# A prologue's order of steps: V weights later in TensorE's queue, the second weight spread as a step

## Chip, cores and metric

One core of a Trainium2 chip. The metric is the device time of one execution in microseconds; the time before is the median of 4 runs, 819.42 us (818.78 to 820.4). One execution was profiled.

## What is computed

x is 2048 tokens by 640, bf16. It is layer-normalised, goes through 32-head attention (20 channels a head) and through a gated unit, and both are combined with x:

```
xn  = layernorm(x)
q, k, v = xn @ wqkv                    # 32 heads of 20
s   = softmax(q k^T / sqrt(20)) v @ wo
g   = silu((sigmoid(xn @ w_gate) * (xn @ w_up)) @ w_down)
out = x + s * g
```

## The kernel before

The heads are taken in 8 groups of four (`GH`), the queries in 4 chunks of 512 tokens; a block is one group with one chunk. The kernel has two stages.

**The prologue** (the `with` that begins at line 259) normalises all of x, transposes it, and makes for group 0 the whole of K, the first chunk of Q, and V of tokens 0 to 1023 (for groups 0 and 1). Tokens lie in 16 tiles of 128; four tiles make a chunk. Transfers are issued by SyncE (SP) at lines 263 to 267: tiles 0 to 7, the q and k weights of group 0 (`wst`), tiles 8 to 15, the V weights (`wv0`). Everything else is a list of steps written out by hand, `PRO` (line 76): each entry names an engine, a step and its numbers, and line 404 issues them one after the other. Within an engine the list is the order of execution (the engines named in `manual_schedule`); an engine waits at a step until that step's inputs are there, whatever stands behind it. The steps:

- `st k` (lines 320 to 332): mean and variance of tile k, on VectorE (DVE) by two batch-norm statistics and an aggregate, or on ScalarE (ACT) by two activations with sums.
- `rs g` (334): reciprocal deviations of tiles 2g and 2g+1, on GpSimd (POOL); `xn k` (341): the normalised tile, on DVE.
- `tr k` (348): five 128x128 transposes on TensorE (PE) into one of four buffers `tp`; `ev k` (353): its copy into `xnT`, on ACT or DVE.
- `k c` (357): K of chunk c, five matmuls of 512 columns into the one buffer `pk`; `km c` (361): its largest absolute value per row, DVE; `kt c` (366): its copy to `kT`, ACT, behind `km c` by a wait on the same buffer. `k c+1` needs both done.
- `v c i` (379): V of two tiles, ten matmuls of 160 columns with `wv0` into one of two buffers `pv`; `ve c i` (383): its copy, ACT.
- `q`, `abs`, `mdp`, `md`, `bound`, `qe0` (369 to 397): the first chunk of Q, its absolute value, a bound on the scores from the largest k, and the copy of q. `qe0` is the last step; the first scores need it.
- `w0`, `idt`, `ones`, `consts`, `more1`, `more2`: constants on POOL; `warm` (315): 28 matmuls on tile 4 whose result is not used.
- `spread` (291): POOL copies the landed `wst` of group 0 into the padded tile `wqks[0]` that `k` and `q` read. `spread_wst` (187) and `load_wst` (181) do this for any group; `wst` has one buffer.

**The loop** (line 1063 on) is planned in Python while the program is built: a model of engine times, which starts at zero whatever the prologue took, hands out scores, exponentials, products with V, the gated unit and the output projection. The instruction order that comes of it is fixed. In its first round, at block 0, it calls `spread_wst(1, load_wst(1))` (line 1137). POOL and SP are not under the manual order there; in the built program this copy stands on POOL right behind `more2`, ahead of `rs 5`, `rs 4`, `rs 7` and `rs 6`, and its two transfers stand on SP right behind `wv0`.

Of the kernel before, what the change touches and what calls it, by code (L numbers as in the profile page):

```python
# [13 lines left out]
ACT = mybir.ActivationFunctionType  # L14
# [12 lines left out]
PG = 2  # L27
# [47 lines left out]

PRO = (
    ("ACT", "table"), ("POOL", "w0"), ("POOL", "idt"), ("POOL", "more1"), ("ACT", "st", 0), ("DVE", "st", 1),
    ("POOL", "ones"), ("POOL", "consts"), ("DVE", "st", 2), ("DVE", "st", 3), ("ACT", "st", 4), ("PE", "warm"),
    ("DVE", "st", 5), ("POOL", "rs", 0), ("ACT", "st", 6), ("DVE", "st", 7), ("POOL", "rs", 2), ("DVE", "xn", 1),
    ("DVE", "xn", 0), ("POOL", "rs", 1), ("PE", "tr", 1), ("DVE", "xn", 4), ("ACT", "st", 9), ("PE", "tr", 0),  # L80
    ("DVE", "xn", 5), ("PE", "tr", 4), ("DVE", "ev", 1), ("PE", "tr", 5), ("POOL", "rs", 3), ("DVE", "ev", 0),
    ("DVE", "xn", 2), ("PE", "v", 0, 0), ("DVE", "xn", 3), ("ACT", "ev", 4), ("POOL", "spread"), ("DVE", "st", 11),
    ("PE", "tr", 3), ("ACT", "ev", 5), ("PE", "tr", 2), ("DVE", "xn", 6), ("POOL", "more2"), ("ACT", "ev", 3),
    ("PE", "v", 1, 0), ("DVE", "st", 10), ("ACT", "ev", 2), ("PE", "tr", 6), ("ACT", "st", 15), ("DVE", "st", 13),
    ("PE", "q"), ("POOL", "rs", 5), ("DVE", "xn", 7), ("PE", "k", 0), ("DVE", "st", 8), ("ACT", "ve", 1, 0),
    ("ACT", "ev", 6), ("PE", "tr", 7), ("DVE", "xn", 11), ("POOL", "rs", 4), ("PE", "v", 0, 1), ("ACT", "ve", 0, 0),
    ("DVE", "km", 0), ("ACT", "ev", 7), ("DVE", "xn", 10), ("PE", "tr", 11), ("ACT", "kt", 0), ("DVE", "st", 14),
    ("PE", "v", 1, 1), ("ACT", "ve", 0, 1), ("ACT", "st", 12), ("PE", "k", 1), ("DVE", "xn", 8), ("POOL", "rs", 7),
    ("DVE", "ev", 11), ("DVE", "xn", 9), ("PE", "tr", 8), ("DVE", "km", 1), ("PE", "tr", 10), ("PE", "tr", 9),
    ("ACT", "ev", 8), ("DVE", "xn", 15), ("POOL", "rs", 6), ("DVE", "ev", 10), ("ACT", "kt", 1), ("PE", "tr", 15),  # L90
    ("DVE", "ev", 9), ("ACT", "ve", 1, 1), ("DVE", "xn", 14), ("ACT", "ev", 15), ("PE", "k", 2), ("DVE", "xn", 13),
    ("DVE", "xn", 12), ("ACT", "abs"), ("PE", "tr", 13), ("DVE", "km", 2), ("PE", "tr", 14), ("ACT", "ev", 13),
    ("PE", "tr", 12), ("DVE", "ev", 14), ("ACT", "kt", 2), ("DVE", "ev", 12), ("DVE", "mdp"), ("PE", "k", 3),
    ("DVE", "km", 3), ("ACT", "kt", 3), ("DVE", "md"), ("PE", "bound"), ("DVE", "qe0"),
)

LOG2E = 1.4426950408889634
# [14 lines left out]
def kernel(  # L112
# [68 lines left out]
    def load_wst(g):  # L181
        st = wk.tile([P, KD, 2, GC], BF16, tag="wst", bufs=1, name="wst")
        for t in range(2):
            nc.sync.dma_start(out=st[:, :, t, :], in_=wqkv_v[:, :, t, g * GC:(g + 1) * GC])
        return st

    def spread_wst(g, st):
        nc.gpsimd.tensor_copy(out=wqks[g % 2][:, :, :, 1:1 + DH],
                              in_=st.rearrange("p kd t (j e) -> p (kd t) j e", e=DH))
# [4 lines left out]
    def load_wv(pr):  # L194
        w = wk.tile([P, KD, 2 * GC], BF16, tag="wv", bufs=1, name="wv")
        nc.sync.dma_start(out=w, in_=wqkv_v[:, :, 2, pr * 2 * GC:(pr + 1) * 2 * GC])
        return w
# [61 lines left out]
    with tc.tile_pool(name="ln", bufs=2) as lp, \  # L259
# [14 lines left out]
        mdp = lp.tile([P, P], BF16, tag="mdp", bufs=1, name="mdp")  # L274
# [16 lines left out]
        def s_spread(eng):  # L291
            spread_wst(0, wst0)

        def s_consts(eng):
            nc.gpsimd.memset(vts[0].rearrange("p t h c -> p (t h) c")[:, :, 0:1], 1.0)
            nc.gpsimd.memset(esum, -1.0)
            esum_v = esum.rearrange("p (j i) -> p j i", i=32)
            nc.gpsimd.affine_select(out=esum_v, in_=esum_v, compare_op=ALU.is_ge, fill=0.0,
                                    base=0, pattern=[[-32, GH], [-P, 32]], channel_multiplier=1)
            nc.gpsimd.affine_select(out=esum_v, in_=esum_v, compare_op=ALU.is_ge, fill=0.0,  # L300
                                    base=31, pattern=[[32, GH], [P, 32]], channel_multiplier=-1)
# [94 lines left out]
        def s_qe0(eng):  # L396
            q_evac(pq[0], qts[0])

        nc.vector.memset(eps_t, 0.0)
        nc.vector.memset(mhalf, -0.5)  # L400
        steps = dict(table=s_table, idt=s_idt, w0=s_w0, ones=s_ones, spread=s_spread, consts=s_consts, more1=s_more1,
                     more2=s_more2, warm=s_warm, st=s_st, rs=s_rs, xn=s_xn, tr=s_tr, ev=s_ev, k=s_k, km=s_km, kt=s_kt,
                     mdp=s_mdp, md=s_md, v=s_v, ve=s_ve, q=s_q, abs=s_abs, bound=s_bound, qe0=s_qe0)
        for eng, name, *args in PRO:
            steps[name](eng, *args)

# [60 lines left out]
    def gc(b):  # L467
        if b < PAIR:
            return divmod(b, NQC)
        return NG - 2 + (b - PAIR) % 2, (b - PAIR) // 2  # L470
# [348 lines left out]
    for b in range(NBLK):  # L819
        g, c = gc(b)  # L820
# [242 lines left out]
    with tc.manual_schedule(engines={ENG.PE, ENG.Activation, ENG.DVE}):  # L1063
# [64 lines left out]
        while chain or items or glu_items or o_next < NQC or any(it.i < len(it.ops) for it in active):  # L1128
# [3 lines left out]
            if bb > blk_loaded:  # L1132
                blk_loaded = bb
                rule.update(zip(KEYS, PLAN[bb]) if bb < len(PLAN) else ())
                g, c = gc(bb)
                if c == 0 and g + 1 < PG:
                    spread_wst(g + 1, load_wst(g + 1))
                if c == 0 and g + 1 < NG:
                    if g % 2 == 1:
                        wvs[(g + 1) // 2] = load_wv((g + 1) // 2)  # L1140
# [39 lines left out]
            for eng in ("ACT", "DVE"):  # L1180
# [67 lines left out]
                elif pass_ok:  # L1248
                    dve_last = "pass"
                    d = dve_pass[0]  # L1250
                    k = d["k"]
# [199 lines left out]
```

## Time and profile before

| | |
|---|---|
| median of 4 runs | 819.42 us |
| profiled execution | 818.78 us |
| its span, first to last instruction | 816.8 us |
| PE, DVE, ACT, POOL busy | 776.1, 785.7, 782.9, 82.2 us |
| first scores start | 31.39 us |
| granted TensorE clock, mean | 0.993 |

Times in rows are microseconds from the span's start. In a timeline row the first number is the start, the second how long the group lasted, and the bracket holds the idle time of the engine before it and what ended it. In the chain of waits, each piece is a start, a length and what ran. In a table of windows each stretch has the busy time (and count) of PE, weight loads, DVE, ACT and POOL, then the granted clock, the transfer engines' share and GB/s. L numbers are lines of the kernel.

### The profile page before, as it was taken

The numbers are of one execution on the slowest core, as the hardware profiler recorded it, in microseconds if no ns is written. First come the engines' busy times: TensorE is split into PE (matmuls) and PEld (weight loads), VectorE is DVE, ScalarE is ACT, GpSimd is POOL, SyncE is SP. The second block draws the span as 40 slices with busy tenths as digits, with TensorE's granted clock in tenths as the row PEclk, the third lists the DMA queues.
The fourth block names the chain that finished last, engine by engine and source line by source line (L and its number), as shares of the span: only waits on it lengthen the run. The fifth ranks groups of instructions, "written<-read, shape, count | busy, mean of one in ns | idle before, by whom it ended". The sixth has DMA issues, their size and how long they took to land.

```text
span 816.8 us, 17041 instructions
## 1 busy us (share of the span) xinstructions
PE 776.1 (95%) x6456; PEld 271.7 (33%) x6456; DVE 785.7 (96%) x1244; ACT 782.9 (96%) x1008; POOL 82.2 (10%) x99
## 2 busy tenths in 40 slices
PE   5799999999999999999999999999999999998996
PEld 5433333333323323333333222333332223233332
DVE  7899999999999999999999999999999999998993
ACT  7899999999999999999999999999999999998991
POOL 6000000001000000000000010000000003022041
PEclk9999999999999999999999999999999999999999
DMA  5431311133222222322122222334121334315031
GB/s 159 138 79 51 100 38 36 41 76 84 66 68 70 60 56 73 81 56 76 46 59 65 71 84 62 85 111 118 44 86 40 93 90 133 98 54 149 25 101 40
DMA packets 95874, 62.57 MB, mean 77 GB/s; under 512 B 36388, under 2 KB 89684, under 8 KB 95792
## 3 DMA queue, kind: packets, MB, share of 16 engines
q1 hardware_dynamic: 95504, 61.16, 26.9%
q8 instruction: 50, 0.82, 0.4%
q14 instruction: 32, 0.26, 0.1%
q10 hardware_dynamic: 288, 0.33, 0.1%
HBM read 47.82 MB, written 13.63 MB: 75 GB/s over the span
## 4 chain that ended last, share of the span: by engine, by line
ACT 38%; PE 28%; DVE 25%; issue 5%; DMA 2%; SPq 1%; POOL 0%; DVEq 0%; ACTq 0%; POOLq 0%
ACT pt L142 35%; DVE iv L1239 9%; PE scA L885 8%; PE bk L921 6%; PE bk L694 5%; DVE pb L967 5%; PE bk L732 4%; DVE pb L961 3%; DVE pb L964 3%; ACT tnh L142 2%; PE bk L885 1%; PE bk L554 1%; SPq L264 1%; DVE hT L702 1%; PE bk L662 1%
## 5 line engine op out<-in xcount | busy, mean ns | idle before, releaser
L142 ACT ACTIVATE pt<-scA 128x1024 bf16<-128x1024 f32 x685 | 696.8, 1174 | 4.3 <-PE bk L885 2.9
L1239 DVE TENSOR_SCALAR iv<-bk 128x512 int16<-128x512 f32 x504 | 330.8, 678 | 2.8 <-PE bk L885 2.3
L885 PE MATMUL scA<-q,kT 32*128 32x512 bf16 x1368 | 266.5, 383 | 10.1 <-ACT pt L142 6.3
L885 PE MATMUL bk<-q,kT 32*128 32x512 bf16 x680 | 207.6, 382 | 3.2 <-DVE iv L1239 1.8
L921 PE MATMUL bk<-pt,v 128*21 128x512 bf16 x1544 | 181.3, 382 | 0.1
L885 PEld LDWEIGHTS <-kT 32*128 32x128 bf16 x2048 | 82.6, 91 | 260.8 <-issue 249.2
L967 DVE TENSOR_TENSOR pb<-iv,pb 128x2048 bf16<-128x2048 bf16 x126 | 158.8, 1260 | 0.6
L921 PE MATMUL bk<-pb,v 128*21 128x512 bf16 x1008 | 156.7, 382 | 0.7 <-DVE pb L961 0.2
L694 PE MATMUL bk<-xnT,wgu 128*128 128x512 bf16 x520 | 144.5, 382 | 2.5 <-DVE iv L1239 1.2
L142 ACT ACTIVATE pt<-bk 128x512 bf16<-128x512 f32 x176 | 130.5, 741 | 3.5 <-PE bk L885 3.4
L951 POOL TENSOR_TENSOR on_bf<-on,rl 128x512 bf16<-128x512 f32 x31 | 42.5, 1371 | 649.3 <-DMA rl<-rd 344.4
L961 DVE TENSOR_SCALAR pb<-iv 128x2048 int16<-128x2048 int16 x126 | 92.5, 734 | 0.2
L964 DVE TENSOR_SCALAR pb<-iv 128x2048 int16<-128x2048 int16 x126 | 92.1, 731 | 0.0
L732 PE MATMUL bk<-wd,hT 128*128 128x320 bf16 x448 | 85.8, 305 | 2.3 <-DVE otmp L795 1.6
L921 PEld LDWEIGHTS <-v 128*21 128x21 bf16 x2552 | 48.6, 90 | 93.7 <-issue 76.6
L694 PEld LDWEIGHTS <-wgu 128*128 128x128 bf16 x520 | 39.2, 97 | 64.3 <-issue 42.4
L732 PEld LDWEIGHTS <-hT 128*128 128x128 bf16 x448 | 35.8, 97 | 45.3 <-issue 35.1
L554 PE MATMUL bk<-xnT,wu 128*128 128x512 bf16 x160 | 44.9, 382 | 0.5 <-DVE iv L1239 0.2
L142 ACT ACTIVATE tnh<-bk 128x512 bf16<-128x512 f32 (+1 forms) x56 | 42.5, 760 | 0.1
L702 DVE SCALAR_TENSOR_TENSOR hT<-tnh,bk 128x512 bf16<-128x512 bf16 x52 | 35.2, 677 | 1.3 <-ACT tnh L142 0.6
L662 PE MATMUL bk<-wv,xnT 128*128 128x160 bf16 x280 | 26.6, 234 | 0.8 <-DVE iv L1239 0.4
L798 POOL TENSOR_TENSOR xnT<-otmp,xnT 128x320 bf16<-128x320 f32 x24 | 20.4, 865 | 56.6 <-DVE otmp L795 31.2
(111 smaller groups left out, 372.2 us busy)
## 6 DMA issues: line engine op xcount, KB each, us to landing
rl<-rd SPq DMA_DIRECT2D x124, 64.0 KB
wgu<-in_B_w_gate_dram SPq DMA_DIRECT2D x24, 320.0 KB
wgu<-in_B_w_up_dram SPq DMA_DIRECT2D x24, 320.0 KB
gq_dram<-gqs SPq DMA_DIRECT2D x24, 160.0 KB
xnT<-gq_dram SPq DMA_DIRECT2D x12, 320.0 KB
xt<-in_A_x_dram SPq DMA_DIRECT2D x16, 160.0 KB
oD<-on_bf SPq DMA_DIRECT2D x124, 20.0 KB
wd<-in_B_w_down_dram SPq DMA_DIRECT2D x1, 2080.0 KB
```

Of the source, the lines that this page charges most:

```text
L142: return nc.scalar.add_instruction(mybir.InstActivation(func=func, name=nc.get_next_instruction_name(), engine=ENG.Activation, ins=[nc.sca ...
L554: nc.tensor.matmul(st["ps"], lhsT=wus[u][:, kd, i, :], rhs=xnT[:, c, kd, :], start=(kd == 0), stop=(kd == KD - 1))
L694: nc.tensor.matmul(st[key][0:fs, :], lhsT=w[:, i, kd, ko * P:ko * P + fs], rhs=xnT[:, c, kd, :], start=(kd == 0), stop=(kd == KD - 1))
L702: nc.vector.scalar_tensor_tensor(out=hT[0:fs, kf, :], in0=st["t"][0:fs, :], scalar=1.0, in1=st["u"][0:fs, :], op0=ALU.add, op1=ALU.mult)
L732: nc.tensor.matmul(st["ps"][:, 0:HD], lhsT=hT[0:fsz[kf], kf, t4 * P:(t4 + 1) * P], rhs=wd[0:fsz[kf], kf, h * HD:(h + 1) * HD], start=(kf = ...
L885: nc.tensor.matmul(dst, lhsT=kTs[gc(b)[0] % 2][32 * j:32 * j + 32, kt * P:(kt + 1) * P], rhs=qts[b % 3][32 * j:32 * j + 32, :], start=True ...
L921: nc.tensor.matmul(bank[pv_bank[0]][32 * j:32 * j + DH + 1, :], lhsT=lhsT, rhs=u["src"], start=first, stop=last, tile_position=(0, 32 * j) ...
L951: nc.gpsimd.tensor_tensor(out=on_bf, in0=on, in1=rl, op=ALU.mult)
L961: nc.vector.tensor_scalar(out=pb[:, 0, :, :].bitcast(I16), in0=iv, scalar1=0x7F80, scalar2=1, op0=ALU.bitwise_and, op1=ALU.bitwise_or)
L964: nc.vector.tensor_scalar(out=pb[:, 1, :, :].bitcast(I16), in0=iv, scalar1=0x007F, scalar2=0x3F00, op0=ALU.bitwise_and, op1=ALU.bitwise_or)
L967: nc.vector.tensor_tensor(out=pb[:, 1, :, :], in0=iv.bitcast(BF16), in1=pb[:, 1, :, :], op=ALU.mult)
L1239: nc.vector.tensor_scalar(out=d["iv"][:, j, :], in0=bank[bk], scalar1=B_OFF, scalar2=0.0, op0=ALU.add, op1=ALU.max)
```

## The change

The list `PRO` is replaced by another order of the same steps with one step more, `spr1`, which calls `spread_wst(1, load_wst(1))`; the call in the loop goes. The old and the new order, engine by engine (the table load on ACT left out):

```
PE before: warm tr1 tr0 tr4 tr5 v00 tr3 tr2 v10 tr6 q k0 tr7 v01 tr11 v11 k1 tr8 tr10 tr9 tr15 k2
           tr13 tr14 tr12 k3 bound
PE after:  warm tr0 tr1 tr2 tr3 tr5 tr4 k0 q v01 tr7 tr6 v10 tr8 k1 tr9 tr10 tr11 v11 tr15 k2
           tr13 tr14 tr12 v00 k3 bound
ACT before: st0 st4 st6 st9 ev4 ev5 ev3 ev2 st15 ve10 ev6 ve00 ev7 kt0 ve01 st12 ev8 kt1 ve11 ev15
            abs ev13 kt2 kt3
ACT after:  st0 st3 st6 st8 ev3 ev2 ev1 st10 ev4 ev5 abs kt0 ev6 st12 ev9 ve10 ev10 kt1 ve01 ve11
            ev15 ev13 kt2 ve00 kt3
DVE before: st1 st2 st3 st5 st7 xn1 xn0 xn4 xn5 ev1 ev0 xn2 xn3 st11 xn6 st10 st13 xn7 st8 xn11 km0
            xn10 st14 xn8 ev11 xn9 km1 xn15 ev10 ev9 xn14 xn13 xn12 km2 ev14 ev12 mdp km3 md qe0
DVE after:  st1 st2 st4 st5 st7 xn0 xn1 xn2 xn3 st9 xn5 xn4 ev0 st13 st14 xn6 xn7 km0 st11 xn8 ev7
            xn9 st15 xn10 xn11 ev8 km1 xn15 ev11 xn14 xn13 xn12 km2 ev14 ev12 mdp km3 md qe0
POOL before: w0 idt more1 ones consts rs0 rs2 rs1 rs3 spread more2 (copy for group 1) rs5 rs4 rs7 rs6
POOL after:  w0 idt more1 ones consts rs0 rs1 rs2 spread rs3 more2 rs4 spr1 rs5 rs7 rs6
```

The rest of the diff:

```diff
+        def s_spr1(eng):
+            spread_wst(1, load_wst(1))
+
...
-        steps = dict(table=s_table, idt=s_idt, w0=s_w0, ones=s_ones, spread=s_spread, consts=s_consts, more1=s_more1,
...
+        steps = dict(table=s_table, idt=s_idt, w0=s_w0, ones=s_ones, spread=s_spread, spr1=s_spr1, consts=s_consts,
...
-                if c == 0 and g + 1 < PG:
-                    spread_wst(g + 1, load_wst(g + 1))
```

In the built programs the order of SP is the same in both, and PE, ACT and DVE have the same order from the first scores on.

## The prediction

> **What bounds the kernel now.** I read the page's sums first, then the chain that ended last in order of time up to the first scores, then the timeline of that stretch engine by engine, and last the table of windows for the clock. The page:
>
> ```profile
> span 816.8 us, 17041 instructions
> ...
> PE 776.1 (95%) x6456; PEld 271.7 (33%) x6456; DVE 785.7 (96%) x1244; ACT 782.9 (96%) x1008; POOL 82.2 (10%) x99
> ...
> PE   5799999999999999999999999999999999998996
> ...
> DVE  7899999999999999999999999999999999998993
> ACT  7899999999999999999999999999999999998991
> ```
>
> Three engines are full from the second slice to the last two. The diff cannot touch that part: the instruction order of PE, ACT and DVE from the first score on, and all of SyncE's order, are the same in both programs once line numbers are left out; only the prologue, some 31 us, differs. So the question is when the first scores (31.39) come. The chain up to there:
>
> ```profile
> 9.60 4.05 DMA wv<-in_A_wqkv_dram
> ...
> 13.69 1.23 PE psv L244 x10
> 14.92 1.07 PE tp L351 x10
> 15.98 1.33 PE psv L244 x10
> ...
> 24.27 0.60 ACT kT L210
> ...
> 24.91 1.24 PE psk L202 x5
> ...
> 30.64 0.70 DVE q L239
> ```
>
> The chain runs through the landing of the V weights: `v 0 0` is PE's fifth prologue step after the warm-up, and everything behind it on PE waits although its own inputs are there. The timeline shows what the wait holds up (last bracket: idle time and what ended it):
>
> ```profile
> 13.69 1.23 PE L244 MATMUL psv<-wv,xnT 128*128 128x160 bf16 x10 [2.49 <-DMA wv<-in_A_wqkv_dram]
> 15.49 1.29 ACT L354 COPY xnT<-tp 128x640 bf16<-128x640 bf16 x2 [2.58 <-PE tp L351]
> 19.91 0.69 DVE L363 TENSOR_REDUCE mk<-psk 128x1 f32<-128x512 f32 x1 [2.04 <-PE psk L202]
> ```
>
> PE stands 2.49 us, ACT 2.58 (ev 3 waits for tr 3 behind it), DVE 2.04 (km 0 waits for k 0 behind all). One stall, seen three times. And it has a second price:
>
> ```profile
> 13.00:14.00 1.00, 0.31 (x5) 0.31 (x5) 0.97 (x4) 0.00 (x0) 0.61 (x1) 1.00 0.71 118
> 14.00:15.00 1.00, 1.00 (x11) 1.00 (x9) 0.97 (x4) 0.00 (x0) 0.00 (x0) 0.51 0.67 99
> 15.00:16.00 1.00, 1.00 (x12) 1.00 (x10) 0.97 (x4) 0.51 (x1) 0.53 (x1) 0.50 0.00 0
> 16.00:17.00 1.00, 1.00 (x10) 1.00 (x9) 1.00 (x3) 1.00 (x3) 0.92 (x3) 0.50 0.00 0
> ```
>
> The third column from the end is the granted clock: half from 14.01 to 17.42, so the V matmuls there start every 133 ns instead of 69, the transposes every 107 instead of 56.
>
> **How I work out the new order.** I walk the step list: each engine takes its steps in order, a step starts at the later of "engine free" and "inputs there plus 0.045". Time an engine spends per step, from start to start in the rows: DVE st 0.99, xn 0.36, ev 0.40, km 0.61; ACT st 1.94, ev and kt 0.58, ve 0.31, abs 0.55 (record 0.63); PE at full clock tr 0.28, v 0.69, k and q 1.08; POOL rs 1.02, spread 0.85 to 1.05. The records of the last instruction end 0.1 to 0.2 later, which the dependants see. Landings are the trace's: tiles 3, 6, 8, 9 at 5.26, 7.20, 9.19, 9.70, wst at 8.63, wv at 13.65. The same walk on the old order, with its clock drop, ends q at 31.36; the trace has 31.33 (30.64 + 0.69). So the method is good to some tenths.
>
> **The tail is the same in both.** From the start of k 2 both lists run k 2, km 2, kt 2, k 3, km 3, md, bound, qe0. Before: 24.91 to 31.33, 6.42 us. New in it are only `v 0 0` ahead of k 3 and `ve 0 0` ahead of kt 3. PE stands 0.81 before k 3 (27.80, it waits for kt 2) and v takes 10 x 0.069 = 0.69; ACT stands 2.06 before kt 3 and ve takes 0.31. Both at nothing; without that cover they would cost 0.69 and 0.31. So what counts is the start of k 2, which waits for kt 1.
>
> **ACT sets it.** In the new order ACT does st 0, 3, 6, 8 back to back: 5.26 + 3 x 1.94 = 11.1 (tile 8 lands at 9.19, when st 8 is due at 9.2: no slack). Then ev 3 waits for tr 3, due at 11.34 (xn 3 at 10.42). From 11.39 ACT never stands: 3 ev to 13.13, st 10 to 15.07, ev 4, ev 5 to 16.23, abs 16.78, kt 0 17.36, ev 6 17.94, st 12 19.88, ev 9 20.46, ve 20.77, ev 10 21.35, kt 1 read out at 22.04. k 2 at 22.08, against 24.91: **2.83 us sooner**. It holds if the inputs are there. DVE, from 8.77 without a pause: 12 xn of 0.36, five st (9, 13, 14, 11, 15) 4.95, three ev 1.20, km 0 0.61, and 0.58 lost on one xn (below) sum to 11.6, so km 1 starts at 20.4 and ends at 21.06, 0.29 ahead of kt 1. PE: tr 5 12.25, tr 4, k 0 13.28, q 14.36, v 0 1 15.44 (weights landed 1.8 earlier, so their wait is gone and not moved), k 1 18.12, tr 10 19.75. Its slack is 0.2 at tr 9, 0.5 at km 0.
>
> **Part by part.** Six st stay on ACT and ten on DVE, so those only change places. One ev goes from DVE to ACT: +0.58 and -0.40, inside the sums above. Taking V out of PE's head: the gain. `spr1`: the transfers and their place in SyncE's queue are the same in both built programs, and so is the wait for the first spread to free the buffer; that ends near 10.3 instead of 12.2, so the 200 KB leave sooner beside the last tiles. If they share the engines, at 200 KB over the 290 GB/s of those slices, tiles 13 to 15 come up to 0.7 late; they land at 12.19, 12.63 and 13.09 and are used at 12.87, 13.86 and 18.27: nothing. Nothing follows on SyncE until 30.37. On POOL the copy stood before rs 5 in the old program too (15.47, after 1.86 of waiting), and now stands behind rs 4 as well, before rs 5, 7, 6: rs 5 needs st 11, at 17.3, so nothing; if the weights landed after 17.3, their delay would come through.
>
> **Clock, row against rule.** The page TensorE: Matmul & The Clock Gate of the Trainium skill ("Why this matters for your kernels") asks for no PE-idle gap over about 3 us. Here a gap of 2.49 was enough: in 10.60 to 14.01 PE's records cover 0.27 of the window, and the next ran at half. By the rule the old order would have kept its clock, its walk ends at 30.34 and the gain is 1.8; by the rows it is 2.8. I take the rows. In the new order the same window holds 0.69 of PE work (longest gap 1.1 us, before tr 5). Covers of 0.48 (27.67 to 31.08) kept full clock, 0.52 near 741 lost it, so 0.69 should keep it, with little margin. Bounds: 0 and, if 14.01 to 17.42 drops all the same, 1.16 (q doubles, abs and kt 0 follow, walk ends at 29.73).
>
> **Port, row against rule.** xn 3 took 1012 ns instead of 437 while POOL's weight copy ran (11.14 to 12.19). The new copy, at 9.35, falls on xn 2: 0.58 on DVE, of which ACT sees 0.2; bounds 0 and 0.6. SBUF — State Buffer ("Who interferes with whom") makes the second of the two block fully, for any GpSimd instruction. The rs steps speak against taking it so: beside their powers (8.42 to 10.36) four xn took 395 to 442 ns, and POOL's stretched from 707 to 875 and 941. By the rule about five xn of the new order, near rs 1, 3, 5, 7 and 6, lose up to 0.7 each, 3.5 in all; by the rows nothing. I take the rows.
>
> **Sum.** 2.83 from the walk, 2.8 taken. The profiled execution took 818.78 around its span of 816.8, so 816.0 there; that run is the fastest of four, the median 819.42 lies 0.64 above it. From the median: **816.6**.
>
> **Rivals.** *Clock drops anyway* (14%): for it, that window phases differ between runs and the margin is small; 816.6 + 1.16 = 817.8. *The loop gives it back* (12%): some wait in the loop is tied to a landing, not to the first score. Against it: the first gate weights are issued at 30.37, 0.2 after md, so they move with it, and ACT stands only 4.3 and DVE 2.8 us before their two largest rows in 816.8; then 819.4, no change. *POOL's port lock* (6%, slower): the five blocked xn above, on DVE between 8.8 and 20.4, where the new order has no idle time. DVE has 0.29 to spare against ACT and 2.83 to lose, so it turns slower from 3.1 us; at 3.5 it is 819.8, and worse if PE's gaps then also halve the clock (+1.2, 821.0). My own case has 68%.
>
> **Range.** Low end: 816.0 less 0.7 for a lucky loop, 815.3. High end: the clock case plus the 0.64 that separates runs, 818.5; it also holds late tiles (tiles 3 and 8 later by 1.0 cost 2.0 in the walk, since st 3 now heads ACT's queue). Faster by over 0.2% (1.64 us, below 817.78; about what a measurement can tell from no change): my case and half the clock case, 0.75; within: 0.19; slower: 0.06.
>
> **What would show it.** In the new profile: no wait of PE for wv; ACT without idle from about 11.4 to 22; the third k near 22.1 and q's end near 28.5; clock 1.00 in the windows from 11 to 28; the loop's length unchanged. Wrong if k 2 comes on time and the span does not follow, if a half-clock stretch appears before 20, or if xn rows near rs run to 0.7 us or more.

## The result

The changed kernel takes 818.12 us (median of 43 runs, 815.25 to 823.18) where the kernel before takes 820.19 (64 runs, 817.08 to 824.83): a ratio of 0.9977 [0.9968, 0.9986], or 1.9 us less (2.1 between the two medians). That is a small gain, but clear of the noise. The median lies inside the range, and the gain is two thirds of the 2.8 us that the forecast gave. The kernel was also run a second time, unchanged, with one group of the experiments; there it had 0.9988 [0.9971, 1.0005].

The one profiled execution of the changed kernel took 820.48 us, 2.4 over its median and 1.7 over the profiled execution before. It is a good witness of where work stands and a bad one of the total. The page:

```profile
span 818.5 us, 17043 instructions
...
PE 779.5 (95%) x6456; PEld 272.4 (33%) x6456; DVE 785.2 (96%) x1243; ACT 784.1 (96%) x1009; POOL 83.8 (10%) x99
...
PE   6899999999999999999999999999999999998996
```

ACT has one instruction more and DVE one less (the copy that changed engines). PE has as many as before and is busy 3.4 us longer: the same matmuls, some of them slower. The chain of waits, in order of time:

```profile
9.32 0.98 DVE xn L348
...
12.17 0.70 ACT xnT L358
...
14.20 2.19 PE psk L203 x5
16.40 1.93 PE psq L228 x5
...
23.71 0.60 ACT kT L211
...
24.36 1.24 PE psk L203 x5
...
30.08 0.70 DVE q L240
```

The landing of the V weights, 4.05 us of this chain before, is gone from it, and `q` ends at 30.78 instead of 31.33. But the third k starts at 24.36, not at 22.08 as forecast. The chain says where the 2.3 us are: k 0 and q take 2.19 and 1.93, where a k took 1.24 before, and one xn takes 0.98. The timeline of PE shows the same with the idle time:

```profile
12.92 1.29 PE L355 MATMUL tp<-ident,xn 128*128 128x128 bf16 x10 [0.78 <-ACT xnT L358]
14.11 2.29 PE L203 MATMUL psk<-xnT,wqk 128*128 128x512 bf16 x5
...
20.38 1.24 PE L203 MATMUL psk<-xnT,wqk 128*128 128x512 bf16 x5
```

Until about 18 PE runs at half speed: ten transposes in 1.29 instead of 0.72, k 0 in 2.29 instead of 1.24. No step of it waits for the V weights. The slow stretch comes before the first entry of the granted clock (the column reads 1.00 there, by default); only the lengths of the rows tell it. A second slow stretch is in the clock column, at the start of the loop (columns as in the table of windows before):

```profile
32.00:33.00 1.00, 1.00 (x9) 0.93 (x8) 1.00 (x3) 1.00 (x3) 0.00 (x0) 0.50 1.12 334
33.00:34.00 1.00, 1.00 (x9) 0.42 (x7) 0.28 (x1) 0.82 (x1) 0.00 (x0) 0.50 0.80 205
34.00:35.00 1.00, 1.00 (x11) 0.89 (x8) 0.69 (x1) 0.75 (x2) 0.00 (x0) 0.50 0.91 273
```

The clock's records put it at 31.64 to 35.05: in that stretch it is half, PE is full and DVE and ACT stand: 0.28 of DVE busy in one microsecond. In the kernel before this stretch was at full clock, and PE did 16 matmuls in the second of these rows where it now does 9:

```profile
32.00:33.00 1.00, 0.69 (x8) 0.48 (x7) 1.00 (x3) 1.00 (x2) 0.00 (x0) 1.00 1.06 307
33.00:34.00 1.00, 1.00 (x16) 0.64 (x14) 0.85 (x3) 1.00 (x2) 0.00 (x0) 1.00 1.05 295
34.00:35.00 1.00, 1.00 (x17) 0.87 (x15) 1.00 (x2) 1.00 (x3) 0.00 (x0) 1.00 0.76 206
```

### The profile page after: what moved, and what is told of

The parts are those of the page before. It is cut to its first block, busy times and chain, and to the rows that moved or that the text cites. A ratio compares the mean times of both kernels' runs of the same rounds, so it can differ in the third digit from the quotient of the medians.

```text
span 818.5 us, 17043 instructions
## 1 busy us (share of the span) xinstructions
PE 779.5 (95%) x6456; PEld 272.4 (33%) x6456; DVE 785.2 (96%) x1243; ACT 784.1 (96%) x1009; POOL 83.8 (10%) x99
## 4 chain that ended last, share of the span: by engine, by line
ACT 39%; PE 29%; DVE 24%; issue 4%; DMA 2%; SPq 1%; POOL 0%; DVEq 0%; ACTq 0%; POOLq 0%
ACT pt L143 35%; DVE iv L1241 9%; PE scA L889 8%; PE bk L925 6%; DVE pb L971 5%; PE bk L736 4%; PE bk L698 4%; DVE pb L965 3%; DVE pb L968 3%; ACT tnh L143 2%; PE bk L792 1%; PE bk L666 1%; PE bk L889 1%; DVE hT L706 1%; PE bk L558 1%
```

## The experiments

The theory after the result: the walk is right in its mechanism, and what is missing went into two places, VectorE steps held up beside GpSimd, and TensorE's clock, in the prologue and above all at the start of the loop. Rivals: the gain comes from something else than the V weights (the new order as a whole), or the loop gives part of it back by a wait that has nothing to do with the clock. Seven further kernels and the changed one again were run, in two groups of four, each group beside runs of the kernel before: 820.48 (21 runs) and 819.83 (17 runs). No run takes `spr1` alone.

**The order before, with V moved alone.**

```
  PE:  v 0 0 from behind tr 5 to ahead of k 3;  v 1 0 from behind tr 2 to behind tr 7
  ACT: ve 0 0 to ahead of kt 3;  ve 1 0 to behind kt 0
```

> The old order with V alone moved: v 0 0 ahead of k 3 with its copy ahead of kt 3, v 1 0 behind tr 7 with its copy behind kt 0. Nothing else differs. If taking V out of PE's head is what the change lives on, PE no longer waits for the V weights and the last prologue step ends near 29.7 in the trace (31.3 before), 1.6 us below the kernel before, more than half of the new order's gain. If the rest of the new order makes the gain, it stays within 0.5 us of the kernel before.

Measured: 818.86 us (12 runs), ratio 0.9982 [0.9966, 0.9998]. PE's timeline:

```profile
15.31 1.24 PE L202 MATMUL psk<-xnT,wqk 128*128 128x512 bf16 x5
...
20.54 1.24 PE L202 MATMUL psk<-xnT,wqk 128*128 128x512 bf16 x4
...
30.21 0.39 PE L885 MATMUL scA<-q,kT 32*128 32x512 bf16 x2 [0.79 <-DVE q L239]
```

The first k starts 3.3 us sooner than before (18.63), and the first scores come at 30.21 for 31.39. Taking V out of PE's head brings most of what the whole change measures, 0.18% of 0.23%; the intervals overlap, so that the rest of the reordering adds nothing can't be said, only that it isn't needed for most of the gain. The interval ends just under 1, and the profiled execution itself is level with the one before (818.66 and 818.78): this loop, too, begins at half clock, from 31.83 to 35.24.

**The order before, with PE kept busy while it waits for the V weights.** Nothing is moved; 40 unused 128-column matmuls on tile 4 stand ahead of `v 0 0`.

```
+ ("PE", "fill", 40), ("PE", "v", 0, 0),
```

> The old order with 40 small matmuls, whose result nobody reads, in PE's queue right ahead of v 0 0, so that PE works while it waits for the V weights. The wait for the weights stays. If the half clock behind the wait is a part of the old order's price, the windows from 14 to 17.4 show clock 1.00, the last prologue step ends near 30.4 instead of 31.3, and the time falls by about 1.0 us. If only the wait counts, nothing moves (within 0.4 us).

Measured: 817.05 us (10 runs), 0.9957 [0.9942, 0.9973]: 3.5 us less where 1.0 was expected. In its profile the clock is full from 9.78 on, and the first scores come at 30.93, 0.46 before the old ones. So the clock is worth something in the prologue, but most of this gain doesn't come from there. The expectation missed by 2.5 us. The profile can't show where the rest is: it is the slowest of the ten runs, 818.90.

**The changed kernel, kept warm in its prologue.** Six more warm-up matmuls, and 4, 4, 4, 8 and 4 unused ones behind `tr` 0, 1, 2, 3 and 5.

> The new order with PE kept at work on matmuls that nobody reads: 34 instead of 28 in the warm-up, and 4, 4, 4, 8 and 4 behind tr 0, 1, 2, 3 and 5. If the new order loses its gain to a clock that the transposes do not release (the profiled execution ran at half until 17.98), the first k and q run at full clock, the last prologue step ends near 28.8 to 29.3 instead of 30.8, and the median falls by 1 to 1.5 us below the new order's (near 816.8 where the new order has 818.1). If the clock is a side matter, it equals the new order, or is slower by the 0.3 us by which the extra work can delay tr 5.

Measured: 814.64 us (6 runs), 0.9921 [0.9894, 0.9947], where some 816.8 was expected. The profiled execution is the slowest of the six, 817.46. In it k 0 takes 1.24 and the first scores come at 29.04, 1.79 before those of the changed kernel's profile. But the loop begins at half clock here too:

```profile
29.00:30.00 1.00, 0.96 (x8) 0.24 (x8) 0.76 (x2) 0.18 (x1) 0.00 (x0) 0.50 0.75 192
30.00:31.00 1.00, 0.92 (x9) 0.63 (x6) 1.00 (x3) 1.00 (x2) 0.00 (x0) 0.50 1.14 338
```

**The changed kernel, kept warm at the bound.** 18 unused matmuls between k 3 and `bound`, 12 between `bound` and the first scores, in stretches in which PE waits for DVE.

```
- ("DVE", "md"), ("PE", "bound"),
+ ("DVE", "md"), ("PE", "fill", 18, "pv"), ("PE", "bound"), ("PE", "fill", 12, "pv"),
```

> The new order with 18 matmuls that nobody reads between k 3 and bound and 12 between bound and the first scores. If the clock that fell to half at the start of the loop (31.64 to 35.05 in the profiled execution) is a part of the time, that stretch keeps clock 1.00 and the median falls by 0.5 to 1.0 us below the new order's 818.1. If PE is not the bound there or the stretch is rare, it equals the new order within 0.3 us.

Measured: 814.41 us (6 runs), 0.9919 [0.9896, 0.9943]: 3.7 under the changed kernel, where 0.5 to 1.0 was expected. The prologue is nothing special (clock half from 13.31 to 16.72, first scores at 30.08), but the loop starts at full clock:

```profile
32.00:33.00 1.00, 1.00 (x14) 0.66 (x12) 0.83 (x2) 1.00 (x3) 0.00 (x0) 1.00 1.14 343
33.00:34.00 1.00, 1.00 (x14) 0.64 (x12) 1.00 (x3) 1.00 (x3) 0.00 (x0) 1.00 1.10 269
34.00:35.00 1.00, 0.91 (x10) 0.58 (x11) 1.00 (x2) 1.00 (x3) 0.00 (x0) 1.00 0.68 195
```

PE does 14 matmuls in each of the first two rows, 9 in the same rows of the changed kernel, and DVE and ACT are all but full.

**The changed kernel again, unchanged.** For its spread, and for a second profile.

> The new order unchanged, beside the next three on one chip. Ratio to the kernel before 0.9977 if it is what it was; a second trace shows another phase of the clock's windows.

Measured: 818.83 us (12 runs), 0.9988 [0.9971, 1.0005]. The second profile is nearer to the walk. PE:

```profile
13.39 1.24 PE L203 MATMUL psk<-xnT,wqk 128*128 128x512 bf16 x4 [0.16 <-ACT xnT L358]
14.46 1.24 PE L228 MATMUL psq<-xnT,wqk 128*128 128x512 bf16 x5
...
22.69 1.25 PE L203 MATMUL psk<-xnT,wqk 128*128 128x512 bf16 x4
...
29.18 0.39 PE L889 MATMUL scA<-q,kT 32*128 32x512 bf16 x2 [0.79 <-DVE q L240]
```

(A count of x4 means that one record is missing; a k has five matmuls.) Here the clock is full from 10.41 on, k 0 and q take 1.24, and the first scores come 1.65 before those of the first profile. It then loses the clock from 30.89 to 34.30. So the same program came out of its prologue at two times, 29.18 and 30.83, and both profiles enter the loop at half clock.

**Both fills in the changed kernel.**

> The new order with the fill matmuls of both earlier runs: 34 in the warm-up, behind tr 0 to tr 3 and tr 5, and around bound. If each held the clock in its own stretch, the clock is 1.00 from 9 or 11 us to 730, the last prologue step ends near 29, and the median falls below both (814.6 and 814.4) by about 1 us, to some 813.5. If the two earlier gains had one cause, it equals them.

Measured: 816.71 us (6 runs), 0.9955 [0.9938, 0.9971], where 813.5 was expected; both kernels with one part of the fills have lower medians. In its trace the clock is full from 10.00 to 805.3 without a break, and `q` ends at 28.76: the walk said 28.57. So the prediction's walk is right to 0.2 us when the clock is there. What the clock theory can't say is why this kernel isn't ahead of the one with fills at the bound alone.

**The order before, kept warm at the bound.**

> The old order with 18 and 12 matmuls that nobody reads around bound. If the clock at the start of the loop is what the ends of both orders pay for, the median falls by 0.5 to 1.0 us (half of the executions losing 1 to 1.5 us), less than the 3.7 us that the same edit seemed to bring in the new order; by as much as there if another thing than the clock is at work in that edit.

Measured: 816.60 us (6 runs), 0.9952 [0.9935, 0.9969], with the first scores at 31.62, 0.2 later than before. The profile before showed no half clock at the start of the loop; for all that 0.48% comes off, 3.2 us by the medians where 0.5 to 1.0 was expected. That is nearly what the same edit brought in the new order (3.7), so by the expectation's own terms another thing than the clock at the loop's start is at work.

**The changed kernel, transposes at the bound in place of matmuls.** As the fills at the bound, with 18 and 12 transposes of tile 4.

> The new order with 18 and 12 transposes instead of the matmuls around bound. If transposes count as work for the clock like matmuls, it equals new_fill_end (ratio 0.992). If they count little, as the long half-clock stretch of the profiled execution under 25 transposes suggests, it equals the new order (0.9977).

Measured: 814.02 us (6 runs), 0.9930 [0.9906, 0.9954]; full clock at the loop's start, first scores at 29.80. Transposes held the clock there as matmuls did. Against the order before with fills at the bound, in the same group of runs, the new order is 2.6 us ahead by the medians (816.60 and 814.02), and 1.8 by the ratios (0.9952 and 0.9930) and by the first scores (31.62 and 29.80). The two ratios' intervals overlap (0.9954 and 0.9935 are their inner ends), and the new order with both fills isn't ahead at all (816.71), though its first scores come at 28.90. So the forecast's 2.8 is not shown by a comparison with the clock treated alike; what is found lies between nothing and 2.6.

**What a half-clock start of the loop costs.** From the start of the first exponential to that of the 41st, as the traces have it:

```
before                34.55      changed               35.45
old, 40 fills         34.55      changed, again        35.67
changed, at bound     34.55      old, V moved          35.67
old, at bound         34.55      changed, kept warm    34.98
changed, both         34.55
changed, transposes   34.55
```

The six traces whose loop starts at full clock agree to 0.01 us, the four others are 0.43 to 1.12 later. That settles the price and, with it, the rival of a wait in the loop that has nothing to do with the clock: in this stretch there is none. Between there and 725 us, all at full clock, the other nine loops drift against that of the kernel before by up to 1.9 us, in both directions; the cause of that is open.

**What stays open.** The kernels with fills are 3.1 to 6.1 us under the kernel before by the medians, and the clock at the loop's start is 1.1 of it at most. Part of the rest is a stall late in the loop, where DVE waits for the gate's rows read back from memory (`gq_dram`) and ACT for PE. The rows for 725 to 760 and for two microseconds of it, first of the changed kernel kept warm in its prologue, then of the changed kernel with transposes at the bound:

```profile
725.00:760.00 35.00, 32.69 (x251) 12.58 (x251) 29.95 (x49) 30.92 (x41) 8.36 (x9) 0.90 0.35 102
740.00:742.00 2.00, 2.00 (x11) 0.64 (x8) 1.23 (x2) 1.33 (x3) 2.00 (x3) 0.50 0.38 112
```

```profile
725.00:760.00 35.00, 32.86 (x272) 13.29 (x271) 33.06 (x54) 33.37 (x45) 7.48 (x9) 1.00 0.35 103
740.00:742.00 2.00, 2.00 (x27) 0.62 (x28) 2.00 (x5) 2.00 (x4) 1.34 (x2) 1.00 0.43 127
```

DVE's idle time in the 35 us is what its busy time leaves: 5.05 and 1.94 us; in the kernel before it is 4.41. Over all ten profiles, DVE stands 1.58 to 2.88 there in the four kernels with work around the bound, 4.41 to 5.31 in the other six. So against the kernel before 1.5 to 2.8 us of their gain are found here, 700 us after the edit. The clock is a part of this too. In all six without work around the bound it is half near 740, for 3.41 us (before, and the first profile of the changed kernel) or 6.83 (the rest). Of the four with such work three keep full clock, and the fourth, the changed kernel with matmuls at the bound, loses it for 3.41 and is the one that stands 2.88. Of DVE's idle time 0.50 to 2.32 us lie inside these half-clock stretches. The wait comes first: in the 3.41 us ahead of each of the seven falls PE's records cover 0.44 to 0.58, and in the three kernels that keep the clock the least covered such piece has 0.62. Why they are better covered there isn't known, and three against one are few. The number of instructions on PE as such doesn't do it: the kernel kept warm has 30 more, as many as the one with fills at the bound, and stands 5.05. Its own 814.64 isn't explained by this stall, as far as the profile of its slowest run can tell. A control with instructions that do next to no work at the head of PE's list was not tried. Each of these is one profile, and among the unprofiled runs of one kernel the times spread over 3 to 8 us.

The mean clock, which every run lists, gives a check on the sum. Half the clock for h microseconds lowers the mean by h / 2 over the run, so h is twice the missing share times the time (it leaves out half clock ahead of the first record, which the mean takes as full: the first profile's 0.991 is its records after 17.98 alone): 18.2 us on average in the kernel before (the runs beside the two groups), 15.2 in the changed kernel (all its runs), 8.2 to 12.3 in the six kernels with fills. Within the runs of the changed kernel a time is 0.27 us longer for each such microsecond. By this slope the 3.0 us less are worth 0.8 of the change's 1.9, and 6 to 10 less are worth 1.6 to 2.7 of what the fills save. That is a correlation (0.66), not an experiment. Kernel by kernel it leaves 0.4 to 4.2 us of their gain; in those with the new order the change's own gain is part of that, the rest is open.

## Why the prediction came out as it did

It named the right mechanism and forecast a gain of 2.8 us where 1.9 was measured. As a ratio the forecast was 0.9966 (816.6 of 819.42), and its rival "clock drops anyway" was 0.9980 (817.8); the measured 0.9977 lies with the rival, and the median is inside the range because the high end was drawn from that rival. Two of its own signs of being wrong came: half clock before 20 in the first profile, and xn rows over 0.7, though beside copies and a memset and not beside the rs steps. Its steps one by one:

- **The V wait is removed and not moved: right.** No V step of the new order waits for its weights, in either profile. V's move alone has 0.9982.
- **ACT sets the pace from 11.4: right when the clock is there.** In the second profile ACT starts its copies at 11.45 after 0.18 of waiting; in the first at 12.17 after 0.98, and it waits another 1.22 for `q` at half clock.
- **The tail from k 2 on is 6.42 long: right to the hundredth.** 24.36 to 30.78. `v 0 0` and `ve 0 0` cost nothing there.
- **`spr1` at nothing for rs 5: right; for DVE: wrong.** POOL's copy waits 1.45 for its landing and rs 5 waits for DVE, as said. But the copy holds up an xn of its own, which the sum left out, though the trace before already had such a row (0.77 at 15.74).
- **The port, one xn of 0.58: the size was off.** DVE's timeline in the first profile, and what POOL did beside it:

```profile
8.96 2.05 DVE L348 TENSOR_SCALAR xn<-xt,mv,rstd 128x640 bf16<-128x640 bf16 x4
...
11.96 1.22 DVE L348 TENSOR_SCALAR xn<-xt,mv,rstd 128x640 bf16<-128x640 bf16 x2
...
15.53 1.06 DVE L348 TENSOR_SCALAR xn<-xt,mv,rstd 128x640 bf16<-128x640 bf16 x2
```

```profile
9.19 0.92 POOL L189 COPY wqk<-wst 128x800 bf16<-128x800 bf16 x1
...
11.75 0.29 POOL L316 CAST ident_f<-ident 128x128 f32<-128x128 bf16 x1
11.98 0.67 POOL L317 MEMSET v<- 128x128 bf16 x1
...
15.21 0.85 POOL L189 COPY wqk<-wst 128x800 bf16<-128x800 bf16 x1 [1.45 <-DMA wst<-in_A_wqkv_dram]
```

  The same stretch of POOL in the second profile, and the pair of xn there:

```profile
12.01 0.40 POOL L316 CAST ident_f<-ident 128x128 f32<-128x128 bf16 x1
12.35 0.87 POOL L317 MEMSET v<- 128x128 bf16 x1
```

```profile
11.86 0.75 DVE L348 TENSOR_SCALAR xn<-xt,mv,rstd 128x640 bf16<-128x640 bf16 x2
```

  An undisturbed four take 1.46, a pair 0.79. Three xn are late, of 980, 871 and 708 ns for 440: 1.2 us in all instead of 0.58. In the second profile it is two, of 976 and 1095, also 1.2. `q` ends at 29.12 there, 0.55 after the walk's end (28.57, which is 29.73 less the 1.16 of the clock case); with one slow xn, in the kernel with both fills, 0.19. The step from one to the other is what the second slow xn costs, as far as two profiles can tell. What the prediction took from the rows against the rule held: beside the powers of the row scales (8.54 to 9.44, 10.46 to 11.22) no xn is slow. It is the copies, and in the first profile a cast or memset, that do it. In all ten profiles together 21 xn take over 500 ns, and every one of them ends 0.18 to 0.22 after a copy or memset of POOL (10.30 after 10.12 for the first of them here). So such an xn is held until POOL's instruction is over, and the price is what is left of that when the xn begins, not a fixed 0.58. In the second profile the pair of xn came first: it kept its 0.75, and cast and memset took 0.40 and 0.87 for 0.29 and 0.67.
- **The clock: the step that failed.** The prediction looked at one window, 10.6 to 14, gave it 0.69 of PE work and said it "should keep" the clock. Two things were wrong. In the first profile the clock had not come up at all by then, and came only at 17.98; the walk took it as full from 10.6 because the trace before had it so. That costs about 1.65 us, the difference between the two profiles' first scores. Where the clock did come up in time, in the second profile, the window held 0.66 of PE work (10.41 to 13.82) and the clock stayed, as the walk had it. And the prediction did not look at the window in which PE waits for the bound, because the row before (0.48 there, clock kept) seemed to clear it. In the new order, in both profiles, the clock is lost there and the loop begins at half: 0.90 and 1.12 us. The rival "clock drops anyway" had the right kind and the wrong place, and its 1.16 was close to the price.
- **The loop's length unchanged: wrong at its start,** by the same 0.90 to 1.12; from there to the end nothing in the order of the size of the change was found that could be laid to it.

For the second profile the terms add up: first scores 2.21 sooner, loop 1.12 later, makes 1.09; the executions differ by 0.84 (817.94 and 818.78). For the first they make a loss of 0.34 (0.56 sooner, 0.90 later), where the execution is 1.70 slower; the other 1.4 lie inside the spread of the runs of one kernel. How often the unprofiled runs lose the clock in which place isn't known; the median's gain of 1.9 lies between what the first profile gives and the forecast.

The Trainium skill (TensorE: Matmul & The Clock Gate, "What's actually happening") has the clock come up after a busy stretch of about 3.4 us and fall after an idle one. The records agree with the length: every stretch of half clock lasts 3.41 or twice that, the last one of the run apart. They don't agree with "busy" and "idle" as a share of PE's records: stretches covered to 0.85 and 0.77 (7.74 to 14.57 in the first profile, cut into pieces of 3.41 us from the first record of the clock backwards) did not bring the clock up, where 0.74 did in the kernel with transposes (12.33 to 15.74); 0.48 kept it in the kernel before, 0.52 lost it in the second profile (27.47 to 30.89), where PE never stood longer than 1.17. No threshold on this share fits all ten profiles, and the runs don't show what would.

## What to carry to other kernels

Taking a late transfer out of an in-order engine's head pays what a walk of the steps says, if the walk's durations hold; check the two things that change durations, the clock and GpSimd's copies beside VectorE, in every stretch that the edit moves, and not only where the old trace showed trouble. A serial tail at the end of a prologue, where PE waits for a few short steps, is the place to look for a clock that falls just as the dense loop begins: some unused matmuls or transposes in PE's waits there cost some 0.2 us here and brought the old order to 0.48% and the changed kernel to 0.45 to 0.81% under the kernel before, where the change alone has 0.23%. Only 0.43 to 1.12 us of that is shown to be the clock at the loop's start. A single profile of a kernel whose runs spread by 1% tells where its work stands; what a change is worth takes the medians.

## What the runs showed that was not expected

- The granted clock's column reads full before its first entry. In the first profile PE ran at half speed until 17.98 with 1.00 in that column; only the matmul rows (2.29 for 1.24) tell.
- The same program came out of its prologue at 29.18 and at 30.83.
- In the four kernels with thirty unused operations at 27 to 31 us a stall near 740 us is 1.5 to 2.8 us shorter, with matmuls and transposes alike. Half clock is part of that stall in the other six and absent in three of these four; why is open.
- The two fastest kernels, 814.02 and 814.41 (6 runs each), are the changed kernel with transposes or matmuls around the bound; both beat the kernel before by 0.7 to 0.8%. Both fills together gave less, 0.45%.
